# Linear attention and a softplus layer on one core: the sums of keys move from TensorE to VectorE, the last tiles are stored whole, and the order is planned anew

## The chip, the cores and the metric

The kernel runs on one core of a Trainium2 chip. The metric is the time of one execution on the device in microseconds (us). The kernel before took 1017.62 us, the median of 3 runs (1016.76 to 1019.33).

The engines are named as in the profile: PE is TensorE (matrix products), PEld its loading of weights, DVE is VectorE, ACT is ScalarE, POOL is GpSimd, and SP is SyncE, which issues all transfers (DMA) here.

## The reference: what is computed

Eight sequences of 576 tokens, with eight heads of 64 channels, go through an attention with 128 random features, and the result through a layer with a softplus:

```python
def phi(x):
    proj = np.einsum('bhsd,md->bhsm', x, omega)
    sq = np.sum(x * x, axis=-1, keepdims=True) / 2.0
    h = proj - sq
    h = h - np.max(h, axis=-1, keepdims=True)
    return np.exp(h) / np.sqrt(m)
q_p, k_p = (phi(q_s), phi(k_s))
kv = np.einsum('bhsm,bhsd->bhmd', k_p, v)
z = np.sum(k_p, axis=2)
num = np.einsum('bhsm,bhmd->bhsd', q_p, kv)
den = np.einsum('bhsm,bhm->bhs', q_p, z)[..., None] + 1e-06
x = num / den                 # 4608 tokens x 512
h = x @ w_in                  # 512 x 2048
g = np.maximum(h, 0.0) + np.log1p(np.exp(-np.abs(h)))
out = g @ w_out               # 2048 x 512
```

All is float32. `z`, the sum of the key features over the 576 tokens of a sequence, is what the change is about.

## The kernel before

**Tiles.** The work of the attention is cut into 16 quads: a quad is four heads of one sequence (`divmod(n, NQ)` gives the sequence and the half). A quad's 576 tokens are five units, four of 128 tokens and one of 64, and these are worked on as (0, 1), (2, 3) and (4). The first sequence (quads 0 and 1, called early) has its own path, in which `v` carries a column of ones, so that its sums of keys come out of the same products as `kv`. The other 14 quads go as follows.

**Keys.** `plan_unit` loads a unit (L375), projects it (L398) or makes the product from high and low halves (L423), takes the maxima (L448, or L440), and exponentiates on ScalarE (L468, L445). The feature tile `ph` has the tokens on the partitions. In `plan_keys`, `add` (L632, L635, L639) sums the units of a quad element by element into one tile `s` of 128 partitions x 512 columns (four heads x 128 features). What is left is the sum of `s` over its partitions. `burst` makes `kv` in one bank (L562) and, in the other half of that bank, the sums: four products with a broadcast column of ones, `one`, as the stationary side and 128 columns of `s` as the moving side (L663). `scaled` (L583) copies all 512 columns of the bank over `s` on ScalarE, times 1/128; `turn` (L575) transposes the `kv` half of it, and `turned` (L580) copies that to `kvs`. `out_z` (L671) sends the two rows of sums to memory, and `in_z` (L675) reads them back spread to all partitions, as `zb`.

**Queries.** `den` (L784) multiplies the query features with `zb` and sums on VectorE, `invert` (L789) takes the reciprocal, `divide` (L793) scales the features, on GpSimd or VectorE. `flip` (L815) transposes them in 32x32 blocks, into a buffer of the kind `flip`, of which there is one; the result goes out to memory (L822, L826) and back in another arrangement (L838). `num` (L864) makes the products with `kvs`, and the pieces `xh` and `xl` (L878, L884) are the input of the layer, in a ring of two blocks of 512 tokens.

**The layer.** `plan_step` does one of 16 slices of 128 hidden channels for a block of 512 tokens: layer 1 with 12 matmuls (L922 to L924: each float32 product is three matmuls of rounded parts), softplus on ScalarE and VectorE (L928, L931, L934, L937), a split into high and low parts (L941, L945), and layer 2 with 12 matmuls (L951 to L953) into four accumulators. There are nine blocks. At the end of a block, for each of its four tiles of 128 tokens, `left` (L985, VectorE) and `right` (L988, ScalarE) copy half a tile each out of the accumulator, and `store` sends it away. The first eight blocks hold the first 512 tokens of each sequence; a tile there is 128 consecutive rows of the output, in one transfer (L993). The ninth block holds the last 64 tokens of all sequences: a tile is twice 64 rows, of two sequences, and it is stored in two transfers of 64 rows (L996).

**Order.** Nothing is scheduled at run time. Each piece of work is declared by `do` with its engine or engines, an estimated duration, a due time, what it comes after, and which buffers it takes and gives. `in_order` goes through them like a simulation: it takes the engine on which something can start first, and of the works that can start there (nearly) at once, the one that is due first. The result is one order for each engine, which the kernel issues. The due times are offsets to the place of the work in the whole (`FIRST`, `NEXT`, `PACE`, `SPREAD`), all of them numbers in the code. `change` is what the planner adds where TensorE goes from full products to products on half its rows or columns and back, and `GLUE` and `HOLD` let it prefer such works one after the other. In the first 70 us `with_fill` puts matmuls that compute nothing (L1100) into TensorE's gaps. Which semaphore waits a work gets follows from the tiles it reads and writes, not from the planner.

Of the kernel before, what the change touches and what calls it, by code (L numbers as in the profile page):

```python
# [10 lines left out]
F32 = mybir.dt.float32  # L11
# [8 lines left out]
P = 128  # L20
# [166 lines left out]
def favor_softplus_kernel(ctx, tc, q0, k0, qx, kx, tx, vv, om, wi, wo, out):  # L187
# [26 lines left out]
    marks = const.tile([P, 16], F32, name="marks")  # L214
    junk = const.tile([P, 1, M], BF16, name="junk")
# [48 lines left out]
    def plan_weights(nm, fc, due):  # L264
# [36 lines left out]
        def low_part(e):  # L301
# [5 lines left out]
            "SP", 1.46, due + 18.22, load, delay=DL, spare=0 if last else 2,  # L307
# [3 lines left out]
        a = do(("ACT", "DVE"), (aw, dw2), due, low_bits, after=[l], port=True)  # L311
        b = do("ACT", aw, due, rebias, after=[l])
# [33 lines left out]
    def plan_unit(q, kind, us, due, early, other=None):  # L346
# [115 lines left out]
        def exponent(j):  # L462
# [9 lines left out]
            "SP", dma(size), due + 7.17, load, behind=prev.get("load"),  # L472
# [7 lines left out]
        if q.b < SPLIT["t" if tail else kind]:  # L480
            r = do("DVE", dve(w), due - 17.18, norms, after=[s], behind=prev.get("norms"), take=sm)
            prev["norms"] = r
            p = do(
                "PE", 0.02 + 0.224 * nt, due - 86.09, project, after=[ld], mode="r",
# [5 lines left out]
            for j in range(2):  # L490
                e = do(
                    "DVE", dve(n // 2 * M), due - 27.10, lambda j=j: maxima(j), after=[p, e], give=[(b, "x")] if j and not early else [],
                )
            e = do("DVE", dve(n), due - 77.06, less_norms, after=[e], port=True)
            e = do("DVE", dve(n), due - 42.60, bias, after=[e], port=True)
            for j in range(2):
                give = [(b, ("ppb", j))]
                es.append(do(
                    "ACT", n // 2 * 0.25, due + 3.35, lambda j=j: exponent(j), after=[e], behind=es[0] if j else None,
                    give=give + ([(b, "sms")] if j else []),  # L500
                ))
        else:
            hs, ls, l = [], [], None
            for j in range(2):
                h = do(
                    ("ACT", "DVE"), (act(w) + 0.1, dve(w, 2) + 0.115), due - 80.15, lambda e, j=j: high(e, j), after=[ld], behind=hs[-1] if hs else None,
                    take=[] if j else [("sp", b, "sps")], port=True,
                )
                hs.append(h)
                l = do(("DVE", "POOL"), (dve(w) + 0.115, pool(w) + 0.05), due - 101.32, lambda e, j=j: low(e, j), after=[h], behind=l, port=True)  # L510
                ls.append(l)
            r = do("DVE", dve(w), due + 37.54, norms, after=[s] + ls, behind=prev.get("norms"), take=sm, give=[(b, "x")])
            prev["norms"] = r
            e, p = None, prev.get("product")
            for t in range(nt):
                p = do(
                    "PE", 0.236, due - 41.99, lambda t=t: product(t), after=ls, behind=p, take=[(kind_, b, ("ppb", t))],
# [3 lines left out]
                    ("ACT", "DVE"), (act(2 * M, PSUM), dve(2 * M)), due - 52.22, lambda e, t=t: first(e, t), after=[p], behind=e,  # L521
                    take=[] if t else phs,
                )
                e = do("DVE", dve(2 * M), due - 55.00, lambda t=t: second(t), after=[c], give=[(b, ("ppb", t))])
            prev["product"] = p
            e = do("DVE", dve(n * M) + 0.07 * (len(to) - 1), due + 148.43, all_maxima, after=[e, r])
            e = do("DVE", dve(n), due - 58.61, less_norms, after=[e], port=True)
            e = do("DVE", dve(n), due - 61.48, bias, after=[e], port=True)
            es = []
            for t in range(nt):  # L530
                es.append(do(
                    "ACT", 0.587, due - 14.73, lambda t=t: exponents(t), after=[e], behind=es[-1] if es else None,
                    give=[(b, "sms")] if t == nt - 1 else [],
                ))
# [9 lines left out]
        for i in range(len(us)):  # L544
            done.append(plan_queries(q, us[i], due - 31.23 * i, b, es, f"{nm}_{i}", 4 * i))
        plan_flip(q, us, due + 45.54 * (len(us) - 1), b, nm, done)

    def plan_keys(q, us, due, b, es, early):
# [36 lines left out]
        def plan_turn(after, give=[]):  # L585
            old = quads[q.n - 2].nums if q.n >= 2 else []
            t = do("PE", 0.15, due - 20.44, turn, after=[after], take=[(any_, q.slots, "kv")], give=give)
            q.kvl = do(
                ("ACT", "DVE"), (act(2 * M, PSUM), dve(2 * M)), due - 51.46, turned, after=[t] + old,
# [4 lines left out]
        if early:  # L594
# [16 lines left out]
            def first_scaled():  # L611
# [4 lines left out]
                "PE", 0.97 if u < 4 else 0.5, due + 30.74, outer, after=es + [q.kvm], give=[(b, "x")],  # L616
                take=[("acc", q.slots, "kt")] if u == 0 else [],
            )
            if u == 4:
                q.kvl = do(  # L620
                    "ACT", act(4 * D + 4, PSUM), due - 3.61, first_scaled, after=[q.kvm], give=[(q.slots, "kt")],
# [4 lines left out]
        def add(e):  # L626
# [16 lines left out]
            ("POOL", "DVE"), (k * pool(w), k * dve(w)), due - 21.75, add, after=es + [q.sum],  # L643
# [9 lines left out]
        def burst():  # L653
# [5 lines left out]
            z = q.bank[:, 2 * M :].rearrange("p (j m) -> p j m", m=M)  # L659
            for j in range(2):  # L660
                for p in range(2):
                    c = 2 * p + j
                    nc.tensor.matmul(  # L663
                        z[p * D : (p + 1) * D, j], one.broadcast_to([P, D]), q.s[:, c * M : (c + 1) * M],
                        start=False, stop=True, skip_group_check=True,
                    )
# [13 lines left out]
        ldv = do("SP", 1.8, due + 54.76, load_v, take=[("v", q.slots, "v")], delay=DL)  # L680
        q.kvm = do(
            "PE", 0.1 + 0.224 * 12, due - 87.62, burst, after=q.es + [ldv, q.sum], take=[(any_, q.slots, "kt")],
            give=[(x, "phs") for _, x in q.units] + [(q.slots, "v")], mode="c",
        )
        a = do("ACT", act(4 * M, PSUM), due + 14.74, lambda: scaled(4 * M), after=[q.kvm], give=[(q.slots, "kt")])
        t = plan_turn(a)
        r = do("SP", 0.55, due - 15.93, out_z, after=[a], delay=DL)
        q.zc = do(
            "SP", 0.73, due + 95.37, in_z, after=[r, t], take=[("zb", q.slots, "zb")], give=[(q.slots, "s")], delay=DL
        )  # L690

    def plan_first(q, u, due, b, es, nm):
# [51 lines left out]
        def x_low():  # L744
# [3 lines left out]
        t = do("PE", 0.13 * n, due - 136.53, turn, after=es, take=[("any", y, "tp")])  # L748
        h = do(("ACT", "DVE"), (act(n * M, PSUM), dve(n * M)), due - 182.81, turned, after=[t], give=[(y, "tp")])
        a = do(  # L750
            "PE", 0.9, due - 137.59, num, after=[h, q.kvl], take=[("any", y, "nb")], behind=q.nums[-1] if q.nums else None,
            give=[(q.slots, "zb")] if u == NU - 1 else [],
        )
        i = do("DVE", 0.25, due - 82.69, invert, after=[a], take=[("dn", y, "dns")], port=True)
        v = do("DVE", dve(4 * D), due - 90.05, divide, after=[i], give=[(y, "nb"), (y, "dns")])
        k = do("PE", 0.28, due - 68.04, back, after=[v], take=[("any", y, "xb")], give=[(b, "x")])
        q.nums.append(a)
        h = do(
            ("DVE", "ACT"), (dve(2 * w), act(2 * w, PSUM)), due + 32.39, x_high, after=[k], take=[("pt", y, "rs")] if u == 4 else [],
# [5 lines left out]
        l = do("DVE", dve(2 * w), due - 55.33, x_low, after=[h], give=[(y, "xb")])  # L765
# [3 lines left out]
    def plan_queries(q, u, due, bu, es, nm, first):  # L769
# [21 lines left out]
        def divide(e):  # L791
# [4 lines left out]
            "DVE", 1.7 if u < 4 else 1.3, due + 51.88, den, after=es + [q.zc], take=[("dn", b, "dns")],  # L796
            give=[(q.slots, "zb")] if u == NU - 1 else [], port=True,
        )
        d = do("DVE", 0.09, due - 62.30, invert, after=[d])
        return do(("POOL", "DVE"), (1.0 * f, dve(n * M)), due + 165.15, divide, after=[d], give=[(b, "dns")], port=True)  # L800

    def plan_flip(q, us, due, bu, nm, done):
# [25 lines left out]
        def back():  # L828
# [12 lines left out]
            "DVE", dve(n * M), due + 11.73, flip, after=done, give=[(bu, "phs")], take=[("flip", b, "vs")], port=True,  # L841
        )
        o = do("SP", 0.6 * n_out, due + 22.70, away, after=[t], give=[(b, "vs")], delay=DL, take=[("fd" if u < 4 else "ft", b, "ds")])
        h = do(
            "SP", 0.6 * n_in, due + 68.16, back, after=[o], delay=DL, behind=prev.get("turn"),
# [8 lines left out]
    def plan_x(q, due, t0, w, any_, qt):  # L854
# [27 lines left out]
        def x_low(p):  # L882
# [4 lines left out]
            "PE", 0.00342 * w + 0.02, due - 97.01, num, after=qt["works"] + [q.kvl],  # L887
# [4 lines left out]
        for p in range(2):  # L892
            h = do(
                ("DVE", "ACT"), (dve(m) + extra, act(m, PSUM) + extra), due - 41.29, lambda e, p=p: x_high(e, p),
                after=[a] + old_reads(t0, m), behind=h,
            )
            l = do("DVE", dve(m), due - 78.05, lambda p=p: x_low(p), after=[h], give=[(y, ("bank", p))])
# [14 lines left out]
    def plan_step(i, t0, n, fc, due, acc, box):  # L912
# [44 lines left out]
        for ccs in ((0, 1), (2, 3)):  # L957
            a = do(
                "PE", 0.70 if n < TB else 1.36, due, lambda ccs=ccs: layer1(ccs), after=[x for cc, x in need if cc in ccs] + [done_w["i", fc]], behind=a,
# [3 lines left out]
        s = do("ACT", act(n, PSUM), due - 38.85, magnitude, after=[a], take=[("u", b, "us")])  # L963
# [244 lines left out]
```

## Time and profile before

| | |
|---|---|
| median of 3 runs | 1017.62 us |
| the profiled execution | 1017.05 us |
| its span, first to last instruction | 1015.3 us |
| granted TensorE clock, mean | 0.998 |
| PE busy | 998.2 us, 98% |
| DVE busy | 717.6 us, 71% |
| ACT busy | 671.3 us, 66% |
| POOL busy | 180.8 us, 18% |
| transfers | 113.78 MB, mean 112 GB/s |

The profile is of one execution. A row of a group names the line of the kernel, the engine, the operation, what it writes and reads, its shape and how often it comes; then busy time and mean nanoseconds of one, and the idle time of its engine just before it with what ended it. A row of a stage gives its start and end, its length, the busy time of PE, PEld, DVE, ACT and POOL with the number of instructions, the granted clock, the mean busy share of the core's 16 DMA engines, and what they moved in GB/s. A row of a wait names who waited for whom: total, times, longest. A row of one line's or one tile's instructions gives shortest, median and longest duration in ns, and first and last start. Matmuls are pipelined: the duration of one is longer than the time for which it holds the engine.

### The profile page before, as it was taken

How to read it: one execution, taken by the hardware profiler on the slowest of the kernel's cores; microseconds unless marked ns; L12 is line 12 of the kernel's file. 1: busy time of each engine (PE TensorE's matmuls, PEld its weight loads, DVE VectorE, ACT ScalarE, POOL GpSimd, SP SyncE). 2: the span in 40 equal slices, each digit the busy share in tenths (PEclk: the TensorE clock that was granted, in tenths of full speed). 3: DMA queues.
4: the chain of work that ended last, by engine and by line, in shares of the span. 5: the costliest groups of instructions: out<-in, count | busy, mean ns of one | idle time of the engine just before them, and what ended most of it. 6: DMA issues, size and time to landing. Idle time of an engine off the chain costs nothing. (4 is left out here: it accounts for less than half of the span.)

```text
span 1015.3 us, 16615 instructions
## 1 busy us (share of the span) xinstructions
PE 998.2 (98%) x5574; PEld 797.7 (79%) x5574; DVE 717.6 (71%) x1880; ACT 671.3 (66%) x1590; POOL 180.8 (18%) x178
## 2 busy tenths in 40 slices
PE   9999999999999999999999999999999999999997
PEld 8777777777777777778778777878778788888886
DVE  7999888888778877778697878787888333223222
ACT  6999777767676767666676767676766444444442
POOL 2123422221123121212041312311212000000000
PEclk9999999999999999999999999999999999999999
DMA  9667354343433333342534243534231301001001
GB/s 354 233 247 265 101 166 135 130 122 116 127 126 126 93 109 104 121 131 73 151 115 149 76 130 104 160 95 128 82 124 47 96 21 42 1 1 42 1 1 41
DMA packets 64172, 113.78 MB, mean 112 GB/s; under 512 B 18236, under 2 KB 36824, under 8 KB 64088
## 3 DMA queue, kind: packets, MB, share of 16 engines
q1 hardware_dynamic: 64088, 112.73, 34.9%
q8 instruction: 44, 0.72, 0.3%
q14 instruction: 40, 0.33, 0.1%
HBM read 85.68 MB, written 27.03 MB: 111 GB/s over the span
## 5 line engine op out<-in xcount | busy, mean ns | idle before, releaser
L951 PE MATMUL acc<-wo,gh 128*128 128x512 f32 x576 | 230.4, 400 | 1.0 <-ACT o L988 1.0
L922 PE MATMUL h<-xh,wi 128*128 128x512 f32 x576 | 228.8, 397 | 1.8 <-DVE u L937 1.8
L923 PE MATMUL h<-xl,wi 128*128 128x512 f32 x576 | 225.3, 391 | 0.6 <-DVE xl L884 0.3
L952 PE MATMUL acc<-wo,gh 128*128 128x512 f32 x576 | 225.2, 391 | 0.0
L953 PE MATMUL acc<-wo,gl 128*128 128x512 f32 x576 | 224.6, 390 | 0.0
L924 PE MATMUL h<-xh,wi 128*128 128x512 f32 x576 | 224.4, 390 | 0.0
L937 DVE SCALAR_TENSOR_TENSOR u<-h,u 128x512 f32<-128x512 f32 x144 | 98.3, 683 | 134.9 <-ACT u L934 134.2
L928 ACT ACTIVATE u<-h 128x512 f32<-128x512 f32 x144 | 86.3, 600 | 161.3 <-PE h L924 152.1
L951 PEld LDWEIGHTS acc<-wo,gh 128*128 128x128 f32 x576 | 108.1, 188 | 32.8 <-issue 9.7
L922 PEld LDWEIGHTS h<-xh,wi 128*128 128x128 f32 x576 | 108.2, 188 | 29.8 <-issue 4.1
L953 PEld LDWEIGHTS acc<-wo,gl 128*128 128x128 f32 x576 | 108.1, 188 | 23.6 <-DVE gl L945 0.2
L924 PEld LDWEIGHTS h<-xh,wi 128*128 128x128 f32 x576 | 108.2, 188 | 23.2
L923 PEld LDWEIGHTS h<-xl,wi 128*128 128x128 f32 x576 | 108.2, 188 | 21.5 <-DVE xl L884 0.6
L952 PEld LDWEIGHTS acc<-wo,gh 128*128 128x128 f32 x576 | 108.4, 188 | 19.0
L941 ACT CAST gh<-u 128x512 fp32r<-128x512 f32 x123 | 76.1, 620 | 53.6 <-PE acc L952 44.4
L945 POOL TENSOR_TENSOR gl<-u,gh 128x512 fp32r<-128x512 f32 x43 | 57.9, 1347 | 230.0 <-ACT gh L941 145.9
L934 ACT ACTIVATE u<-u 128x512 f32<-128x512 f32 x144 | 91.5, 635 | 3.9
L784 DVE CUSTOM_DVE_ANT_0 junk<-phq,zb 128x128 bf16<-128x128 f32 (+1 forms) x228 | 80.5, 353 | 18.2 <-ACT phq L445 3.0
L931 ACT ACTIVATE u<-u 128x512 f32<-128x512 f32 x144 | 91.6, 636 | 2.6
L945 DVE TENSOR_TENSOR gl<-u,gh 128x512 fp32r<-128x512 f32 x101 | 70.7, 701 | 23.1 <-ACT gh L941 22.2
L468 ACT ACTIVATE phk<-ppk,smk 128x128 f32<-128x128 f32 x230 | 63.5, 382 | 22.4 <-DVE smk L460 22.3
L445 ACT ACTIVATE phq<-phq,smq 128x128 f32<-128x128 f32 x194 | 61.9, 394 | 9.6 <-DVE smq L460 9.6
(129 smaller groups left out, 1325.9 us busy)
## 6 DMA issues: line engine op xcount, KB each, us to landing
xk<-kx SPq DMA_DIRECT2D x28, 512.0 KB, 3.6
xq<-qx SPq DMA_DIRECT2D x28, 512.0 KB, 5.3
fdq<-flq SPq DMA_DIRECT2D x28, 512.0 KB, 2.9
qq<-fdq SPq DMA_DIRECT2D x112, 128.0 KB, 3.1
rawi<-wi SPq DMA_DIRECT2D x16, 512.0 KB, 8.4
rawo<-wo SPq DMA_DIRECT2D x16, 512.0 KB, 7.1
out<-o SPq DMA_DIRECT2D x32, 256.0 KB, 2.2
v<-vv SPq DMA_DIRECT2D x14, 576.0 KB
```

Source lines behind the costliest of these rows:

```text
L784: nc.vector.tensor_tensor_reduce(jk[r, c % jk.shape[1]], ph[r, c], q.zb[r, h], 1.0, 1e-6, ALU.mult, ALU.add, dn[r, 0, c : c + 1])
L922: nc.tensor.matmul(b["h"], wh, xh[:, cc, t], start=cc == 0, stop=False)
L923: nc.tensor.matmul(b["h"], wh, xl[:, cc, t], start=False, stop=False)
L924: nc.tensor.matmul(b["h"], wl, xh[:, cc, t], start=False, stop=cc == NCC - 1)
L928: nc.scalar.activation(b["u"], b["h"], AF.Abs)
L931: nc.scalar.activation(b["u"], b["u"], AF.Exp, scale=-1.0)
L934: nc.scalar.activation(b["u"], b["u"], AF.Ln, bias=1.0)
L937: nc.vector.scalar_tensor_tensor(b["u"], b["h"], 0.0, b["u"], ALU.max, ALU.add)
L945: (nc.vector if e == "DVE" else nc.gpsimd).tensor_tensor(b["gl"], b["u"], b["gh"].bitcast(F32), ALU.subtract)
L951: nc.tensor.matmul(acc[tt], gh, w2[fc][:, 0], start=fc == 0, stop=False)
L952: nc.tensor.matmul(acc[tt], gh, w2[fc][:, 1], start=False, stop=False)
L953: nc.tensor.matmul(acc[tt], gl, w2[fc][:, 0], start=False, stop=fc == NFC - 1)
```

## The change

The four products with ones leave `burst`. In their place `s` is transposed on VectorE in 32x32 blocks into a new tile `st` (in the one `flip` buffer), reduced over 32 columns to 16, and, in a small tile `few` that is cleared once at the start, transposed again and added over the four groups of 32 partitions. `out_z` then sends 16 rows of 32 numbers from `few`. `scaled` copies only the 256 columns of `kv`, and comes after the first transpose, since it writes over columns of `s` that the transpose reads.

The tiles of the last block are stored with one transfer each, whose destination is an access pattern of 2 x 64 x 512. For them the planner takes ScalarE's copy as ready with the accumulator and not after VectorE's copy; the copies themselves are the same.

The planner's durations for some works, its due times and its other settings have new numbers.

```diff
-AHEAD = 264.67
+AHEAD = 312.45
-SLOW = 6.04
+SLOW = 10.94
-PATIENCE = {"PE": 0.00, "DVE": 0.00, "ACT": 0.18, "POOL": 15.27, "SP": 5.65}
-LEAN = {"DVE": 0.27, "POOL": 0.00, "ACT": 0.00}
-SPREAD = ((0, 10.51), (13, 28.11))
+PATIENCE = {"PE": 0.00, "DVE": 0.02, "ACT": 0.17, "POOL": 15.27, "SP": 4.12}
+LEAN = {"DVE": 0.56, "POOL": 0.00, "ACT": 0.00}
+SPREAD = ((0, 10.51), (17, 8.16))
-GLUE = 0.00
-HOLD = 0.00
-START_PACE = 5.87
-EARLY_Q = 0.74
+GLUE = 67.48
+HOLD = 0.09
+START_PACE = 5.26
+EARLY_Q = 7.20
...
+    few = const.tile([P, 2, 32], F32, name="few")
...
+    nc.gpsimd.memset(few, 0.0)
...
             products(*units[-1], q.v[:, 16:])
-            z = q.bank[:, 2 * M :].rearrange("p (j m) -> p j m", m=M)
-            for j in range(2):
-                for p in range(2):
-                    c = 2 * p + j
-                    nc.tensor.matmul(
-                        z[p * D : (p + 1) * D, j], one.broadcast_to([P, D]), q.s[:, c * M : (c + 1) * M],
-                        start=False, stop=True, skip_group_check=True,
-                    )
...
+        def flip_sums():
+            q.st = at.tile([P, 4 * M], F32, name=f"st{q.nm}", tag=q.slots["st"], bufs=1)
+            nc.vector.transpose(q.st, q.s)
+
+        def sums():
+            nc.vector.tensor_reduce(few[:, 0, : 4 * M // 32], q.st.rearrange("p (j t) -> p j t", t=32), AX.X, ALU.add)
+
+        def last_sums():
+            a, b = few[:, 0], few[:, 1]
+            nc.vector.transpose(b, a)
+            nc.vector.tensor_tensor(a[:D], b[:D], b[D:], ALU.add)
+            nc.vector.tensor_tensor(b[:32], a[:32], a[32:D], ALU.add)
+            nc.vector.tensor_scalar(b[:32], b[:32], rm, None, ALU.mult)
+
         def out_z():
-            q.zd = dram.tile([2, 2 * M], F32, name=f"zd{q.nm}", tag="zd", bufs=2)
-            nc.sync.dma_start(q.zd, q.s[0 : 2 * D : D, 2 * M :])
+            q.zd = dram.tile([4 * M // 32, 32], F32, name=f"zd{q.nm}", tag="zd", bufs=2)
+            nc.sync.dma_start(q.zd, few[: 4 * M // 32, 1])
...
-        a = do("ACT", act(4 * M, PSUM), due + 14.74, lambda: scaled(4 * M), after=[q.kvm], give=[(q.slots, "kt")])
-        t = plan_turn(a)
-        r = do("SP", 0.55, due - 15.93, out_z, after=[a], delay=DL)
-        q.zc = do(
-            "SP", 0.73, due + 95.37, in_z, after=[r, t], take=[("zb", q.slots, "zb")], give=[(q.slots, "s")], delay=DL
+        z = do(
+            "DVE", dve(4 * M), due - 33.63, flip_sums, after=[q.sum], take=[("flip", q.slots, "st"), ("few", q.slots, "few")], port=True,
         )
+        a = do("ACT", act(2 * M, PSUM), due - 46.64, lambda: scaled(2 * M), after=[q.kvm, z], give=[(q.slots, "kt")])
+        plan_turn(a, [(q.slots, "s")])
+        z = do("DVE", dve(4 * M), due + 5.39, sums, after=[z], give=[(q.slots, "st")])
+        z = do("DVE", 0.55, due - 98.77, last_sums, after=[z], port=True)
+        r = do("SP", 0.55, due - 30.52, out_z, after=[z], give=[(q.slots, "few")], delay=DL)
+        q.zc = do("SP", 0.73, due + 123.44, in_z, after=[r], take=[("zb", q.slots, "zb")], delay=DL)
...
-                for j in range(2):
-                    nc.sync.dma_start(out[(2 * u + j + 1) * S - D : (2 * u + j + 1) * S, :], o["t"][j * D : (j + 1) * D])
-
-            a = do("DVE", 0.34, due + 0.15, left, after=[ends[tt]], take=[("end" if last else "t2", o, "s")])
-            r = do("ACT", 0.27, due - 75.97, right, after=[a], give=[(box, ("acc", i, tt))])
-            do("SP", 0.75 if t0 < B * MAIN else 1.5, due + 0.04, store, after=[a, r], give=[(o, "s")], delay=2.0)
+                nc.sync.dma_start(out.rearrange("(b s) d -> b s d", s=S)[2 * u : 2 * u + 2, S - D :, :], o["t"])
+
+            a = do("DVE", 0.34, due - 2.24, left, after=[ends[tt]], take=[("end" if last else "t2", o, "s")])
+            r = do("ACT", 0.27, due - 105.06, right, after=[ends[tt]] if last else [a], behind=a if last else None, give=[(box, ("acc", i, tt))])
+            do("SP", 0.75, due - 38.80, store, after=[a, r], give=[(o, "s")], delay=2.0)
...
-    FIRST = 109.77
-    NEXT = 61.17
-    PACE = 1.82
+    FIRST = 102.61
+    NEXT = 89.06
+    PACE = 3.07
```

Some 40 further lines change only a duration or a due time (the planner's duration of a half of layer 1 goes from 1.36 to 1.375 us, of a quarter of layer 2 from 0.684 to 0.692, of the burst from 0.1 + 0.224 x 12 to 0.1 + 0.224 x 10).

More of the change, by code (lines that the diff above doesn't have):

```diff
@@ L306, in plan_weights @@
         l = do(
-            "SP", 1.46, due + 18.22, load, delay=DL, spare=0 if last else 2,
+            "SP", 1.46, due + 31.61, load, delay=DL, spare=0 if last else 2,
             take=[({"i": "qh", "o": "ql"}[nm] if last else "w", box, "raw")],
@@ L310, in plan_weights @@
         aw, dw, dw2, pw = act(DM), dve(DM), dve(DM, 2), pool(DM)
-        a = do(("ACT", "DVE"), (aw, dw2), due, low_bits, after=[l], port=True)
-        b = do("ACT", aw, due, rebias, after=[l])
+        a = do(("ACT", "DVE"), (aw + 0.035, dw2), due, low_bits, after=[l], port=True)
+        b = do("ACT", aw + 0.03, due, rebias, after=[l])
         c = do("DVE", dw, due, joined, after=[a, b], port=True)
@@ L471, in plan_unit @@
         ld = do(
-            "SP", dma(size), due + 7.17, load, behind=prev.get("load"),
+            "SP", dma(size), due + 15.20, load, behind=prev.get("load"),
             take=[("w" if early else "x", b, "x")], delay=DL, spare=2 if early else 0,
@@ L480, in plan_unit @@
         if q.b < SPLIT["t" if tail else kind]:
-            r = do("DVE", dve(w), due - 17.18, norms, after=[s], behind=prev.get("norms"), take=sm)
+            r = do("DVE", dve(w), due + 10.58, norms, after=[s], behind=prev.get("norms"), take=sm)
             prev["norms"] = r
             p = do(
-                "PE", 0.02 + 0.224 * nt, due - 86.09, project, after=[ld], mode="r",
+                "PE", 0.02 + 0.224 * nt, due - 96.65, project, after=[ld], mode="r",
                 behind=prev.get("project"),
@@ L491, in plan_unit @@
                 e = do(
-                    "DVE", dve(n // 2 * M), due - 27.10, lambda j=j: maxima(j), after=[p, e], give=[(b, "x")] if j and not early else [],
+                    "DVE", dve(n // 2 * M), due - 36.44, lambda j=j: maxima(j), after=[p, e], give=[(b, "x")] if j and not early else [],
                 )
-            e = do("DVE", dve(n), due - 77.06, less_norms, after=[e], port=True)
-            e = do("DVE", dve(n), due - 42.60, bias, after=[e], port=True)
+            e = do("DVE", dve(n), due - 37.34, less_norms, after=[e], port=True)
+            e = do("DVE", dve(n), due - 45.13, bias, after=[e], port=True)
             for j in range(2):
@@ L498, in plan_unit @@
                 es.append(do(
-                    "ACT", n // 2 * 0.25, due + 3.35, lambda j=j: exponent(j), after=[e], behind=es[0] if j else None,
+                    "ACT", n // 2 * 0.25, due - 0.03, lambda j=j: exponent(j), after=[e], behind=es[0] if j else None,
                     give=give + ([(b, "sms")] if j else []),
@@ L505, in plan_unit @@
                 h = do(
-                    ("ACT", "DVE"), (act(w) + 0.1, dve(w, 2) + 0.115), due - 80.15, lambda e, j=j: high(e, j), after=[ld], behind=hs[-1] if hs else None,
+                    ("ACT", "DVE"), (act(w) + 0.1, dve(w, 2) + 0.115), due - 4.01, lambda e, j=j: high(e, j), after=[ld], behind=hs[-1] if hs else None,
                     take=[] if j else [("sp", b, "sps")], port=True,
@@ L509, in plan_unit @@
                 hs.append(h)
-                l = do(("DVE", "POOL"), (dve(w) + 0.115, pool(w) + 0.05), due - 101.32, lambda e, j=j: low(e, j), after=[h], behind=l, port=True)
+                l = do(("DVE", "POOL"), (dve(w) + 0.115, pool(w) + 0.2), due - 76.28, lambda e, j=j: low(e, j), after=[h], behind=l, port=True)
                 ls.append(l)
-            r = do("DVE", dve(w), due + 37.54, norms, after=[s] + ls, behind=prev.get("norms"), take=sm, give=[(b, "x")])
+            r = do("DVE", dve(w), due + 30.96, norms, after=[s] + ls, behind=prev.get("norms"), take=sm, give=[(b, "x")])
             prev["norms"] = r
@@ L516, in plan_unit @@
                 p = do(
-                    "PE", 0.236, due - 41.99, lambda t=t: product(t), after=ls, behind=p, take=[(kind_, b, ("ppb", t))],
+                    "PE", 0.236, due - 9.84, lambda t=t: product(t), after=ls, behind=p, take=[(kind_, b, ("ppb", t))],
                     give=[(b, "sps")] if t == nt - 1 else [],
@@ L531, in plan_unit @@
                 es.append(do(
-                    "ACT", 0.587, due - 14.73, lambda t=t: exponents(t), after=[e], behind=es[-1] if es else None,
+                    "ACT", 0.587, due - 50.02, lambda t=t: exponents(t), after=[e], behind=es[-1] if es else None,
                     give=[(b, "sms")] if t == nt - 1 else [],
@@ L586, in plan_turn @@
             old = quads[q.n - 2].nums if q.n >= 2 else []
-            t = do("PE", 0.15, due - 20.44, turn, after=[after], take=[(any_, q.slots, "kv")], give=give)
+            t = do("PE", 0.15, due - 81.14, turn, after=[after], take=[(any_, q.slots, "kv")], give=give)
             q.kvl = do(
-                ("ACT", "DVE"), (act(2 * M, PSUM), dve(2 * M)), due - 51.46, turned, after=[t] + old,
+                ("ACT", "DVE"), (act(2 * M, PSUM), dve(2 * M)), due + 3.70, turned, after=[t] + old,
                 give=[(q.slots, "kv")],
@@ L615, in plan_keys @@
             q.kvm = do(
-                "PE", 0.97 if u < 4 else 0.5, due + 30.74, outer, after=es + [q.kvm], give=[(b, "x")],
+                "PE", 0.97 if u < 4 else 0.5, due + 9.14, outer, after=es + [q.kvm], give=[(b, "x")],
                 take=[("acc", q.slots, "kt")] if u == 0 else [],
@@ L620, in plan_keys @@
                 q.kvl = do(
-                    "ACT", act(4 * D + 4, PSUM), due - 3.61, first_scaled, after=[q.kvm], give=[(q.slots, "kt")],
+                    "ACT", act(4 * D + 4, PSUM), due - 59.41, first_scaled, after=[q.kvm], give=[(q.slots, "kt")],
                     take=[("zb", q.slots, "zb")],
@@ L642, in plan_keys @@
         q.sum = do(
-            ("POOL", "DVE"), (k * pool(w), k * dve(w)), due - 21.75, add, after=es + [q.sum],
+            ("POOL", "DVE"), (k * pool(w), k * dve(w) + 0.2), due - 71.26, add, after=es + [q.sum],
             take=[("s", q.slots, "s")] if u == 0 else [], port=True,
@@ L764, in plan_first @@
             return
-        l = do("DVE", dve(2 * w), due - 55.33, x_low, after=[h], give=[(y, "xb")])
+        l = do("DVE", dve(2 * w), due + 7.12, x_low, after=[h], give=[(y, "xb")])
         for p in range(2):
@@ L840, in plan_flip @@
         t = do(
-            "DVE", dve(n * M), due + 11.73, flip, after=done, give=[(bu, "phs")], take=[("flip", b, "vs")], port=True,
+            "DVE", dve(n * M), due + 20.79, flip, after=done, give=[(bu, "phs")], take=[("flip", b, "vs")], port=True,
         )
-        o = do("SP", 0.6 * n_out, due + 22.70, away, after=[t], give=[(b, "vs")], delay=DL, take=[("fd" if u < 4 else "ft", b, "ds")])
+        o = do("SP", 0.6 * n_out, due + 53.49, away, after=[t], give=[(b, "vs")], delay=DL, take=[("fd" if u < 4 else "ft", b, "ds")])
         h = do(
-            "SP", 0.6 * n_in, due + 68.16, back, after=[o], delay=DL, behind=prev.get("turn"),
+            "SP", 0.6 * n_in, due + 4.59, back, after=[o], delay=DL, behind=prev.get("turn"),
             take=[] if qt["works"] else [("q", qt, "tag")], give=[(b, "ds")],
@@ L958, in plan_step @@
             a = do(
-                "PE", 0.70 if n < TB else 1.36, due, lambda ccs=ccs: layer1(ccs), after=[x for cc, x in need if cc in ccs] + [done_w["i", fc]], behind=a,
+                "PE", 0.73 if n < TB else 1.375, due, lambda ccs=ccs: layer1(ccs), after=[x for cc, x in need if cc in ccs] + [done_w["i", fc]], behind=a,
                 take=[] if ccs[0] else [("h", b, "hs")],
```

68 lines of the change are left out of this document (34 added, 34 removed).

## The prediction

> **What bounds the kernel now.** I read the head of the page first, then busy time by stage, then what TensorE (PE) waited for.
>
> ```profile
> span 1015.3 us, 16615 instructions
> PE 998.2 (98%) x5574; PEld 797.7 (79%) x5574; DVE 717.6 (71%) x1880; ACT 671.3 (66%) x1590; POOL 180.8 (18%) x178
> ```
>
> ```profile
> 70.00:90.00 20.00, 20.00 (x126) 15.90 (x125) 19.48 (x52) 19.78 (x46) 6.46 (x6) 1.00 0.86 317
> ...
> 200.00:300.00 100.00, 99.86 (x577) 78.88 (x576) 81.73 (x227) 67.38 (x172) 21.30 (x21) 1.00 0.39 117
> ...
> 950.00:1000.00 50.00, 50.00 (x222) 41.42 (x221) 12.51 (x19) 23.29 (x38) 0.00 (x0) 1.00 0.00 1
> 1000.00:1016.00 16.00, 8.83 (x39) 6.96 (x38) 3.72 (x7) 2.74 (x6) 0.00 (x0) 0.87 0.30 66
> ```
>
> ```profile
> PE ppq L423 <- DVE xl L884: 2.0, 2, 1.2
> PE h L922 <- DVE u L937: 1.8, 3, 0.9
> PE fill L1100 <- ACT xq L705: 1.1, 1, 1.1
> ```
>
> In the stages the columns after the length are busy PE, PE weight load, DVE, ACT and POOL, then clock, DMA share and GB/s. From about 70 us to its last matmul PE has no room: 99.86 of 100 us in the middle, 50 of 50 at the end. VectorE (DVE) is behind it, at 82% in the middle, with 97% only in the lead (19.48 of 20). PE's longest single wait is 1.2 us. So in the body time is set by how much PE has to do, and then a tail follows in which PE does nothing: it works 8.83 of the last 16 us. That tail in order of time, and in slices of half a microsecond:
>
> ```profile
> 1007.68 5.00 SPq L996 DMA_DIRECT2D out<-o  x8
> ...
> 1008.44 0.39 PE L953 MATMUL acc<-wo,gl 128*128 128x512 f32 x1
> 1008.70 0.37 ACT L988 COPY o<-acc 128x256 f32<-128x256 f32 x1 [0.31 <-DVE o L985]
> 1008.87 0.42 DVE L985 COPY o<-acc 128x256 f32<-128x256 f32 x1 [0.25 <-PE acc L953]
> 1009.33 0.37 ACT L988 COPY o<-acc 128x256 f32<-128x256 f32 x1 [0.25 <-DVE o L985]
> ```
>
> ```profile
> 1008.50:1009.00 0.50, 0.33 (x2) 0.00 (x0) 0.25 (x2) 0.30 (x1) 0.00 (x0) 1.00 0.27 66
> ...
> 1010.00:1010.50 0.50, 0.00 (x0) 0.00 (x0) 0.00 (x0) 0.00 (x0) 0.00 (x0) 1.00 0.94 209
> ...
> 1013.50:1014.00 0.50, 0.00 (x0) 0.00 (x0) 0.00 (x0) 0.00 (x0) 0.00 (x0) 0.50 0.86 184
> 1014.00:1014.50 0.50, 0.00 (x0) 0.00 (x0) 0.00 (x0) 0.00 (x0) 0.00 (x0) 0.50 0.02 4
> ```
>
> PE ends at 1008.44 + 0.39 = 1008.83; the span ends 6.5 us later. The last copy is over at 1009.70, and what is left is DMA alone: four tiles of 256 KB in eight halves (1.05 MB) move from about 1008.87 (a share of 0.27 in that half microsecond is 0.13 us at full) to 1014.0, with the engines some nine tenths busy; then 1.3 us to the end.
>
> **Sums of keys leave TensorE.** For each of 14 quads the four products with `one` go, which the trace shows as eight matmuls.
>
> ```profile
> L663 PE MATMUL kt<-s,marks x112: 272/273/273, 69.3 to 756.7; 128*64 128x128 f32 x112
> L583 ACT ACTIVATE s<-kt x14: 581/597/599, 70.7 to 757.6; 128x512 f32<-128x512 f32 x14
> ```
>
> ```profile
> 756.55 0.44 PE kt L663 x8
> ```
>
> The 273 ns are with the pipeline's depth; what eight of them hold up is the 0.44 us of the chain of waits. PE is full at the places from 69 to 757 us, so 14 x 0.44 = **6.2 us** come off the path. The products left in the burst are the same on both sides of the gap, so no further change of array shape goes or comes. ScalarE's `scaled` copies 256 columns instead of 512: 597 ns against 0.37 us for a copy of 128x256 in the tail, 14 x 0.22 = 3.1 us, beside PE's work: nothing on the path.
>
> **What VectorE gets.** Per quad a transpose of 128x512, a reduction of 128x512 to 16, and four small operations.
>
> ```profile
> L815 DVE STREAM_TRANSPOSE flq<-phq 128x1024 f32<-128x1024 f32 x28 | 34.7, 1240 | 0.5
> L388 DVE TENSOR_REDUCE smk<-xk 128x8 f32<-128x512 f32 x28 | 19.0, 678 | 1.7 <-POOL xk L383 1.0 <-ACT xk L381 0.7
> L815 DVE STREAM_TRANSPOSE flq<-phk 128x256 f32<-128x256 f32 x13 | 5.8, 443 | 5.9 <-DMA fdq<-flq 5.8
> L460 DVE SCALAR_TENSOR_TENSOR smk<-smk 128x8 f32<-128x8 f32 x28 | 4.4, 158 | 0.5
> ```
>
> Transpose: a third of the way from 443 to 1240, 0.71. Reduction 0.68. Small ones 4 x 0.16 = 0.64. Together 2.0 us, times 14 = 28 us, between 70 and 760 us: 4 us in each 100, so DVE goes from 82 to 86 of 100. It lies beside PE's work as long as 14 us of each 100 are free; the cover is gone in the lead, where one or two quads (2 to 4 us) meet a DVE that is 97% busy. The new wait is there too: `scaled` overwrites the part of `s` that the transpose reads, so ScalarE waits for DVE, and behind it in ScalarE's queue stand the softplus steps of layer 1 (L928, L931, L934) on which PE's layer 2 waits. The transpose takes the one `flip` buffer, where the flips already wait 5.8 us in all for a DMA to land.
>
> The sums leave for memory behind DVE's work and no longer behind the burst and `scaled`; SP's later loads stand behind that issue, and PE's waits above name no DMA, so I count nothing. The clearing of `few` falls on POOL at the start, which is 18% busy: nothing. That the plan takes the last ScalarE copies as free of DVE's costs and gains nothing, as the two copies themselves are not edited (in the tail each waits for the other, 0.25 us).
>
> **The new order.** Its due times can't be read as time. In the lead, gaps of PE are filled with matmuls that compute nothing, and these count as busy:
>
> ```profile
> L1100 PE MATMUL fill<-ident 128*128 128x128 f32 x56 | 8.5, 290 | 1.1 <-ACT xq L705 1.1
> ```
>
> Bounds: PE stands still 1008.83 - 998.2 = 10.6 us before its last matmul and is filled for 8.5, so no order gains more than 19.1; if each of the 14 quads got one wait as long as PE's longest now, it would lose 14 x 1.2 = 16.8. I take **0**, in the middle of small waits on both sides, and 8 us either way for most of it.
>
> **The last tiles stored whole.** Eight halves, each a run of 64 rows, become four stores of 128 rows. The source has 128 partitions; the destination is now `[2, 64, 512]`, with the 2 outermost, since the two runs of 64 rows lie in different sequences. What the outermost count does must be read from the transfers there are.
>
> ```profile
> DMA packets 64172, 113.78 MB, mean 112 GB/s; under 512 B 18236, under 2 KB 36824, under 8 KB 64088
> ```
>
> ```profile
> xk<-kx SPq DMA_DIRECT2D x28, 512.0 KB, 3.6
> ...
> fdq<-flq SPq DMA_DIRECT2D x28, 64.0 KB, 2.3
> ...
> rest<-r SPq DMA_DIRECT2D x16, 64.0 KB, 2.8
> ...
> zd<-s SPq DMA_DIRECT2D x14, 2.0 KB
> ...
> omf<-om SPq DMA_DIRECT2D x1, 64.0 KB
> ```
>
> The 22 rows of which these are the first and the last count 448 transfers. Packets under 512 B: the two groups with rows of 256 B have (28 + 16) x 256 = 11264 of 18236, which leaves 6972. Sixteen to each transfer (one closing packet for each of 16 engines, as I read it) would be 7168; 196 are missing, 14 x 14. That is the 14 transfers `zd<-s`, whose source is two partitions: two engines each instead of sixteen. It is the only transfer with an outermost count under 16, and the nearest row to a store with a 2 outermost. So I take two engines for the new stores, 64 rows of 2 KB on each.
>
> The Trainium skill, "DMA: Bandwidth & Descriptors", section "Why a DMA increments its semaphore by 16 and not by 1", says that a transfer runs on the largest number of engines up to 16 that divides the slowest dimension of both sides; by it the new store gets two. The same page's list of choices (the row on two transfers to disjoint partition halves) advises one transfer of 128 partitions instead of two halves; by that alone the sum would be the 1008.4 below. `zd<-s` agrees with the first; no run here yet shows a 2 outermost with many rows under it.
>
> The price, from whole tiles in the middle of the run and from the tail now:
>
> ```profile
> 930.50:931.00 0.50, 0.50 (x4) 0.42 (x3) 0.50 (x1) 0.00 (x0) 0.00 (x0) 1.00 1.02 385
> ```
>
> 385 GB/s at a share of 1.02 is 23.6 GB/s for one engine, so 64 rows (131,072 bytes) take 5.55 us. In the tail now, 209 GB/s at 0.94 is 13.9 GB/s, or 9.4 us; there sixteen engines read 64 partitions at once, which two don't, so I take 5.55. All four stores come ready within 2 us, on the same two engines: 4 x 5.55 = 22.2 us from 0.04 after PE's end, then 1.3: a tail of 23.5 instead of 6.5, **+17.0 us**.
>
> **Sum.** The profiled execution took 1017.05 (its span and 1.75 around it), 0.57 under the median of the runs shown. 1017.05 - 6.2 + 0 + 17.0 = 1027.9; I say **1028**.
>
> **The rivals.** *Sixteen engines after all* (spread by the number of rows, which `zd<-s`, with two rows, doesn't exclude): then the last store is issued at 0.89 after PE's end, begins 1.2 later (1007.68 to 1008.87), takes 0.7 (256 KB at the 385 GB/s above) and 1.3 follow, a tail of 4.1. 1017.05 - 6.2 - 2.4 = 1008.4, faster. It decides from four engines up: the sum stands even with before when the tail is 6.5 + 6.2 = 12.7, which leaves 11.4 us for data, and k engines need 44.4 / k. *Two engines at the tail's rate*: 4 x 9.4 = 37.7, tail 39.0, 1043; against it, the 64 partitions shared by sixteen engines. *The new wait*: ScalarE held by a late transpose in every quad, PE without layer 2 work, 16.8 more on top of two engines: 1045; for it, DVE at 97% in the lead and a single flip buffer; against it, PE's waits on DVE of 1.8 and 2.0 in all with DVE at 82%. That the sums don't leave PE, I see no way for.
>
> **Chances.** Two engines 0.70, as all 448 transfers agree with it and one shows it; sixteen 0.17; two engines at the slow rate 0.06; the new wait 0.07. The likeliest one's own range is 1020 to 1036 (8 us of order either way). The range of 1007 to 1036 takes in the sixteen engines too, and leaves out the two slow rivals. A measurement here tells about 0.3%, 3 us, from no change: 1014.6 to 1020.7. Sixteen engines give nearly all of faster, 0.16; their slow end and the fast end of the likeliest give 0.06 within; the rest, 0.78, is slower.
>
> **What will show it.** PE's group L663 gone and PE's last matmul near 1002.6 (the first step); DVE some 28 us up with PE's waits on DVE and ACT small (the second and the order); four stores issued within 2 us of PE's end, and behind them some 22 us in which the DMA share is about 2/16 at 47 GB/s. If that stretch shows a share of 0.9 and ends within 3 us of the last issue, my tail is wrong, and the time is near 1008; if PE ends after 1012, the order or the new wait is.

## The result, and the profile after

The changed kernel took 1033.24 us, the median of 4 runs (1030.81 to 1033.53), against 1018.48 us (4 runs, 1016.76 to 1019.36): a ratio of 1.0142, 95% interval 1.012 to 1.0164. It is slower by some 14.5 us; the forecast was 1028, and the median lies 5.2 us over it. Its profiled execution took 1030.81, with a span of 1029.0; it is the fastest of the four. All ratios below are to the kernel before, run beside on the same chip (its medians there are 1018.05 to 1018.18); the brackets are 95% intervals. A ratio is not exactly the quotient of the two medians.

The head of its page, and its stages (columns as before: busy PE, PEld, DVE, ACT, POOL, then clock, DMA share, GB/s):

```profile
span 1029.0 us, 16459 instructions
PE 990.7 (96%) x5436; PEld 791.2 (77%) x5436; DVE 713.0 (69%) x1860; ACT 684.5 (67%) x1638; POOL 240.3 (23%) x235
```

```profile
150.00:200.00 50.00, 44.09 (x243) 33.24 (x242) 42.51 (x109) 35.65 (x92) 14.36 (x15) 0.93 0.50 150
200.00:300.00 100.00, 100.00 (x562) 78.78 (x561) 76.94 (x209) 70.90 (x178) 32.80 (x31) 1.00 0.36 109
...
950.00:1000.00 50.00, 50.00 (x222) 41.41 (x221) 12.46 (x18) 22.83 (x37) 0.00 (x0) 1.00 0.00 1
1000.00:1030.00 30.00, 5.17 (x23) 3.94 (x21) 2.39 (x5) 1.66 (x5) 0.00 (x0) 0.66 0.10 35
```

PE is full in the middle and at the end, as before, and then works 5.17 of the last 30 us. The end in order of time, and in stretches:

```profile
1004.03 10.23 SPq L1006 DMA_DIRECT2D out<-o  x4
...
1004.79 0.39 PE L964 MATMUL acc<-wo,gl 128*128 128x512 f32 x1
1005.05 0.37 ACT L999 COPY o<-acc 128x256 f32<-128x256 f32 x1 [0.36 <-DVE o L996]
1005.21 0.42 DVE L996 COPY o<-acc 128x256 f32<-128x256 f32 x1 [0.26 <-PE acc L964]
1005.67 0.37 ACT L999 COPY o<-acc 128x256 f32<-128x256 f32 x1 [0.25 <-DVE o L996]
```

```profile
1006.00:1008.00 2.00, 0.00 (x0) 0.00 (x0) 0.00 (x0) 0.04 (x1) 0.00 (x0) 1.00 0.13 31
1008.00:1012.00 4.00, 0.00 (x0) 0.00 (x0) 0.00 (x0) 0.00 (x0) 0.00 (x0) 0.71 0.13 50
...
1020.00:1024.00 4.00, 0.00 (x0) 0.00 (x0) 0.00 (x0) 0.00 (x0) 0.00 (x0) 0.50 0.13 51
1024.00:1028.00 4.00, 0.00 (x0) 0.00 (x0) 0.00 (x0) 0.00 (x0) 0.00 (x0) 0.50 0.10 39
```

PE ends at 1004.79 + 0.39 = 1005.18, 3.7 us earlier than before; the tail is 23.8 us instead of 6.5. For 20 us the sixteen DMA engines are busy for 0.13 of their time, which is two of sixteen, at 51 GB/s.

What VectorE got, and what TensorE waited for:

```profile
L665 DVE STREAM_TRANSPOSE st<-s 128x512 f32<-128x512 f32 x14 | 9.8, 702 | 2.1 <-DMA fdq<-flq 2.1
...
L668 DVE TENSOR_REDUCE few<-st 128x16 f32<-128x512 f32 x14 | 9.6, 684 | 0.2
...
L672 DVE STREAM_TRANSPOSE few<-few 128x32 f32<-128x32 f32 x14 | 2.9, 209 | 0.4
...
L673 DVE TENSOR_TENSOR few<-few 64x32 f32<-64x32 f32 x14 | 2.6, 188 | 0.5
...
L674 DVE TENSOR_TENSOR few<-few 32x32 f32<-32x32 f32 x14 | 2.5, 180 | 0.5
L675 DVE TENSOR_SCALAR few<-few 32x32 f32<-32x32 f32 x14 | 2.4, 170 | 0.5
```

```profile
L585 ACT ACTIVATE s<-kt 128x256 f32<-128x256 f32 x14 | 5.4, 383 | 8.7 <-PE kt L564 7.5 <-DVE st L665 1.2
```

```profile
PE acc L962 <- ACT gh L952: 4.4, 1, 4.4
PE kt L564 <- DVE xl L895: 2.4, 1, 2.4
PE ppq L425 <- DVE phq L438: 1.2, 3, 0.6
```

The new work is 29.8 us of VectorE, yet its total didn't rise (717.6 before, 713.0 now): the new order gives more to GpSimd, 240.3 us instead of 180.8. ScalarE's copy of `kv` (L585) waited 1.2 us in all for the transpose. Two single waits of TensorE, of 2.4 us near 107 us and 4.4 us near 160 us, are new.

The packets answer the count that the prediction made:

```profile
DMA packets 64445, 113.78 MB, mean 111 GB/s; under 512 B 18536, under 2 KB 37096, under 8 KB 64360
```

There are 444 transfers now, four stores for eight. `zd` has 16 rows and so 14 x 16 packets of 128 B. With 11264 packets of 256 B, sixteen closing packets for each of 440 transfers and two for each of the four stores, the sum is 11264 + 224 + 7040 + 8 = 18536, the page's number exactly.

### The profile page after: what moved, and what is told of

Same layout as the page of the kernel before. It is cut to its first block, busy times and chain, and to the rows that moved or that the text cites. A ratio compares the mean times of both kernels' runs of the same rounds, so it can differ in the third digit from the quotient of the medians.

```text
span 1029.0 us, 16459 instructions
## 1 busy us (share of the span) xinstructions
PE 990.7 (96%) x5436; PEld 791.2 (77%) x5436; DVE 713.0 (69%) x1860; ACT 684.5 (67%) x1638; POOL 240.3 (23%) x235
## 2 busy tenths in 40 slices
DMA packets 64445, 113.78 MB, mean 111 GB/s; under 512 B 18536, under 2 KB 37096, under 8 KB 64360
## 4 chain that ended last, share of the span: by engine, by line
PE 76%; DVE 10%; ACT 5%; DMA 4%; issue 2%; POOL 0%; SPq 0%; DVEq 0%; ACTq 0%
PE acc L962 11%; PE h L933 11%; PE h L934 11%; PE h L935 11%; PE acc L963 11%; PE acc L964 11%; PE kt L564 3%; PE ppk L400 3%; PE xp L875 2%; PE ppq L425 2%; DVE junk L795 2%; DMA xq<-q 1%; DMA xq<-qx 1%; DVE flq L826 1%; DVE u L948 1%
## 5 line engine op out<-in xcount | busy, mean ns | idle before, releaser
L956 POOL TENSOR_TENSOR gl<-u,gh 128x512 fp32r<-128x512 f32 x51 | 66.4, 1302 | 231.6 <-ACT gh L952 185.6
L956 DVE TENSOR_TENSOR gl<-u,gh 128x512 fp32r<-128x512 f32 x93 | 66.6, 716 | 25.6 <-ACT gh L952 24.0
L804 POOL TENSOR_TENSOR phq<-phq,dnq 128x512 f32<-128x512 f32 (+1 forms) x57 | 64.0, 1136 | 54.7 <-DVE dnq L800 35.3
```

What stands on the lines that cost most here:

```text
L956: (nc.vector if e == "DVE" else nc.gpsimd).tensor_tensor(b["gl"], b["u"], b["gh"].bitcast(F32), ALU.subtract)
```

## Experiments: the store of the last tiles

**Halves again, in the changed kernel.** The two lines of before come back in `store`:

```diff
-                nc.sync.dma_start(out.rearrange("(b s) d -> b s d", s=S)[2 * u : 2 * u + 2, S - D :, :], o["t"])
+                for j in range(2):
+                    nc.sync.dma_start(out[(2 * u + j + 1) * S - D : (2 * u + j + 1) * S, :], o["t"][j * D : (j + 1) * D])
```

> The changed kernel, with the last four tiles stored as before, in eight halves of 64 rows. If the store with 2 outermost carries the loss, the tail after the last matmul goes from 23.8 us back to 6.5 us, and the time from 1033.2 to about 1016 (its profiled execution from 1030.8 to 1013.5), near the kernel before or under it. If the loss lies in the order or in VectorE's new work, the time stays above 1028.

Measured: 1015.79 us (10 runs), ratio 0.9982 (0.9968 to 0.9996), with a tail of 6.5 us. The rest of the change, by itself, is faster by 1.8 us by the ratio (0.4 to 3.3 by its interval). The store costs 17.4 us by the medians (1033.24 - 1015.79) and 16.3 by the ratios (1.0142 - 0.9982).

**That store alone, in the kernel before.** The same edit the other way round, with the old order and the sums on TensorE.

> The kernel before, with nothing but the store of the last tiles changed to one transfer of 2 x 64 x 512 each. If that store alone costs what the tail showed, the time is 1018 + 17.3 = 1035, with a DMA share of 0.125 for about 21 us after the last matmul. If the long tail needs the new order or the new sums, the time stays at 1018.

Measured: 1033.65 us (4 runs), ratio 1.0158 (1.0142 to 1.0173), which is 16.1 us, with a tail of 23.4 us. Of its stretches after the last matmul:

```profile
1012.00:1016.00 4.00, 0.00 (x0) 0.00 (x0) 0.00 (x0) 0.00 (x0) 0.00 (x0) 0.50 0.13 51
...
1024.00:1028.00 4.00, 0.00 (x0) 0.00 (x0) 0.00 (x0) 0.00 (x0) 0.00 (x0) 0.50 0.13 51
```

Undoing it in one kernel and doing it in the other agree within 2 us: the store is the loss, and it needs nothing else of the change.

**Is it the outermost count?** One transfer of 128 rows and a destination in two levels came together with the 2. In the next kernels the tokens of the last block stand in another order inside a tile, which `plan_rest` arranges when it reads them back, so that the same 128 rows of 2 KB go out with another outermost count:

```diff
-                nc.sync.dma_start(out.rearrange("(b s) d -> b s d", s=S)[2 * u : 2 * u + 2, S - D :, :], o["t"])
+                nc.sync.dma_start(out.rearrange("(b s) d -> s b d", s=S)[S - D :, 2 * u : 2 * u + 2, :], o["t"])
...
+    def in_tiles(x):
+        return x.rearrange("c (u j r) -> c u r j", u=4, j=2)
+
+    def to_tiles(x):
+        return x.rearrange("c (u r j) -> c u r j", u=4, j=2)
...
-                    (nc.scalar.copy if e == "ACT" else nc.vector.tensor_copy)(xh[x], b["t"][:, p])
+                    (nc.scalar.copy if e == "ACT" else nc.vector.tensor_copy)(to_tiles(xh[x]), in_tiles(b["t"][:, p]))
...
-                    nc.vector.tensor_tensor(xl[x], b["t"][:, p], xh[x].bitcast(F32), ALU.subtract)
+                    nc.vector.tensor_tensor(to_tiles(xl[x]), in_tiles(b["t"][:, p]), to_tiles(xh[x].bitcast(F32)), ALU.subtract)
```

> The changed kernel, with the tokens of the last block in another order inside a tile (row r of the two sequences side by side), so that the same tile of 128 rows goes out in one transfer whose destination is 64 x 2 x 512: 64 outermost instead of 2, the same bytes and the same rows of 2 KB. If the outermost count sets how many engines work, all sixteen do: a tail of about 4.1 us, a time of 1033.2 - 19.7 = 1013.5, the DMA share at 0.9. If a destination in two levels as such, or one transfer of 128 rows, is what makes it slow, it stays at 1033.

> The kernel before with the same store of 64 x 2 x 512, and the sums still on TensorE and the old order. If sixteen engines move whole tiles, the tail goes from 6.5 to about 4.1 us and the time from 1018 to 1015.6. If whole tiles gain nothing over halves, 1018.

Measured: in the changed kernel 1014.44 us (6 runs), ratio 0.9964 (0.9949 to 0.998), with a tail of 4.8 us; in the kernel before 1016.65 (10 runs), ratio 0.9982 (0.997 to 0.9995), with a tail of 4.5 us. The end of the first of them:

```profile
1008.00:1009.00 1.00, 0.00 (x0) 0.00 (x0) 0.42 (x1) 0.59 (x2) 0.00 (x0) 1.00 0.92 340
1009.00:1010.00 1.00, 0.00 (x0) 0.00 (x0) 0.00 (x0) 0.00 (x0) 0.00 (x0) 1.00 1.03 383
1010.00:1011.00 1.00, 0.00 (x0) 0.00 (x0) 0.00 (x0) 0.00 (x0) 0.00 (x0) 1.00 0.87 326
```

The destination still has two levels and the transfer still has 128 rows; with 64 outermost it runs on all engines at 383 GB/s. So neither of those made it slow. Two counts between, with tiles of four and of eight sequences (`[4 * g : 4 * g + 4, s0 : s0 + 32, :]` with `s0 = S - D + 32 * h`, and `[:, s0 : s0 + 16, :]` with `s0 = S - D + 16 * u`):

> The changed kernel with tiles of the last block made of 16 rows from each of eight sequences, stored in one transfer of 8 x 16 x 512: 8 outermost. Two engines moved 51 GB/s together, so 25.5 each; eight move 204 GB/s, and four tiles (1.05 MB) take 5.1 us with a DMA share of 0.5. With the 3.2 us that lay around the data in the tail of 2 outermost, a tail of 8.3 us, against 23.8 with 2 and 4.8 with 64 outermost. If anything but the outermost count decides, the tail is 4.8 or 23.8.

> The changed kernel with tiles of the last block made of 32 rows from each of four sequences, stored in one transfer of 4 x 32 x 512: 4 outermost. Four engines at 25.5 GB/s move 102 GB/s: 10.3 us for the four tiles at a DMA share of 0.25, and a tail of about 13.5 us, between 23.8 (2 outermost) and 9.0 (8 outermost). If the engines don't follow the outermost count, it stands near one of these two.

Measured, in a single execution each: 1019.29 us with a tail of 9.0 us (eight) and 1025.74 us with a tail of 14.3 us (four), each tail some 0.7 us over what was expected. Four, then eight:

```profile
1014.00:1016.00 2.00, 0.00 (x0) 0.00 (x0) 0.00 (x0) 0.00 (x0) 0.00 (x0) 0.50 0.26 102
```

```profile
1011.00:1012.00 1.00, 0.00 (x0) 0.00 (x0) 0.00 (x0) 0.00 (x0) 0.00 (x0) 1.00 0.51 180
```

| outermost | DMA share | GB/s | tail, us |
|---|---|---|---|
| 2 | 0.13 | 51 | 23.8 |
| 4 | 0.26 | 102 | 14.3 |
| 8 | 0.51 | 180 | 9.0 |
| 64 | 1.03 | 383 | 4.8 |

The shares are 2, 4, 8 and 16 sixteenths to within 0.03. The packets say the same without any time: those under 512 B are 18536, 18544, 18560 and 18592 in the four kernels. Without the closing packets of the four last stores the count above gives 18528, so the four stores close with 8, 16, 32 and 64 packets: 2, 4, 8 and 16 engines each. The number of engines follows the outermost count of the destination.

## Experiments: the sums of keys and the order

All four are made from the changed kernel with the store of 64 outermost, in the same planned order, so that one thing at a time differs. That reference was run in the section above (0.9964), and once more beside the kernel without VectorE's new work:

> The changed kernel with the store of 64 x 2 x 512 once more, as the reference for the next run on the same chip: 1014.4, ratio 0.9964 to the kernel before.

Measured: 1013.25 us (11 runs), ratio 0.9956 (0.9942 to 0.997). Together the reference is 0.9956 to 0.9964.

**The products in addition.** The eight removed lines with `one` are back in `burst`; nothing reads their results.

```diff
+            z = q.bank[:, 2 * M :].rearrange("p (j m) -> p j m", m=M)
+            for j in range(2):
+                for p in range(2):
+                    c = 2 * p + j
+                    nc.tensor.matmul(
+                        z[p * D : (p + 1) * D, j], one.broadcast_to([P, D]), q.s[:, c * M : (c + 1) * M],
+                        start=False, stop=True, skip_group_check=True,
+                    )
```

> The changed kernel with the store of 64 x 2 x 512 and the four products with ones done in every burst as well, in the same order of work; their results are not read. If TensorE's own time sets the body, they cost 14 x 0.44 = 6.2 us: 1020.6. If the products had lain in time that PE had to wait anyway, nothing: 1014.4.

Measured: 1019.32 us (12 runs, 1016.61 to 1023.12), ratio 1.0009 (0.9996 to 1.0022), 0.0045 to 0.0053 over the reference, which is 4.6 to 5.4 us. By the intervals that is known to some 2 us either way. So they did lie on the path; the 6.2 lies a little higher, but not beyond the intervals.

**VectorE's work left out**, first without and then with the transpose of 128x512:

```diff
-    nc.gpsimd.memset(few, 0.0)
+    nc.gpsimd.memset(few, 1.0)
...
         def flip_sums():
-            q.st = at.tile([P, 4 * M], F32, name=f"st{q.nm}", tag=q.slots["st"], bufs=1)
-            nc.vector.transpose(q.st, q.s)
+            pass
...
         def sums():
-            nc.vector.tensor_reduce(few[:, 0, : 4 * M // 32], q.st.rearrange("p (j t) -> p j t", t=32), AX.X, ALU.add)
+            pass
...
         def last_sums():
-            a, b = few[:, 0], few[:, 1]
-            nc.vector.transpose(b, a)
-            nc.vector.tensor_tensor(a[:D], b[:D], b[D:], ALU.add)
-            nc.vector.tensor_tensor(b[:32], a[:32], a[32:D], ALU.add)
-            nc.vector.tensor_scalar(b[:32], b[:32], rm, None, ALU.mult)
+            pass
```

> The changed kernel with the store of 64 x 2 x 512, in the same order, with the reduction and the four small operations left out, so that the sums of keys are ones and the denominators are wrong; the first transpose stays, and so does what waits for it. VectorE has 14 x 1.4 = 20 us less. If its new work lies beside PE's, the time stays within 1.5 us of 1014.4; if it holds PE up, 4 us or more come back: 1010 or less.

> The same, in the same order, with all of VectorE's new work left out, the transpose of 128x512 too, so that the sums of keys are ones and the denominators are wrong, and ScalarE's copy of kv no longer waits for VectorE. Leaving out the reduction and the four small operations gave 1011.9 against 1014.4 on another chip, 2.5 us for 20 us of VectorE. If that is VectorE's load, the whole of it (2.1 us a quad, 30 us) gives about 3.7: 1010.7. If it is ScalarE's wait for the transpose that costs, another 4 or more come: 1007. If the 2.5 us were the spread of the runs, it stays at 1014.4, within 1 us of the reference.

Measured: 1011.85 us (6 runs), ratio 0.9943 (0.993 to 0.9956) without the five later operations, and 1012.38 (7 runs), ratio 0.9952 (0.9934 to 0.9971), without any of it. The first fell between the two expectations. The second shows no more: 0.9 us by the medians, 0.4 us by the ratios, against a reference on the same chip, inside both intervals. So VectorE's 30 us lie beside PE's work, and neither they nor ScalarE's wait for the transpose cost anything that these runs can tell from nothing, which is about 2 us.

The traces of both also tell where the two new waits of TensorE come from. They are there, as long as ever, when all of VectorE's new work is left out:

```profile
PE acc L957 <- ACT gh L947: 4.4, 1, 4.4
PE kt L564 <- DVE xl L890: 2.4, 1, 2.4
```

So they belong to the new order (which the planner made with this work in it), and not to the time that the work takes.

**The gap near 160 us.**

```diff
-        for w in with_fill(*in_order(works, room, AHEAD, MARGIN), room["any"], 70, fill):
+        for w in with_fill(*in_order(works, room, AHEAD, MARGIN), room["any"], 200, fill):
```

> The changed kernel with the store of 64 x 2 x 512 (median 1014.4, ratio to before 0.9964), and the matmuls that compute nothing put into planned gaps up to 200 us of the plan instead of 70. In the order PE stands for 4.4 us near 160 us, and the granted clock is 0.5 for 6.8 us after it. If the gap is one that the plan itself leaves, and the clock falls because PE stands, the clock stays at 1.0 after it, and 6.8 x 0.5 = 3.4 us come back: near 1011. If the clock falls for another reason, or the gap is no planned one, the time stays at 1014.4.

The gap in the changed kernel, and the same place with the filling:

```profile
160.00:165.00 5.00, 0.89 (x16) 0.70 (x14) 4.84 (x14) 2.30 (x7) 2.13 (x3) 0.81 0.63 210
165.00:170.00 5.00, 4.67 (x20) 3.11 (x22) 4.79 (x14) 3.59 (x12) 0.00 (x0) 0.50 0.02 4
```

```profile
164.06 3.62 PE L1116 MATMUL fill<-ident 128*128 128x128 f32 x30
167.84 0.50 PE L962 MATMUL acc<-wo,gh 128*128 128x512 f32 x1 [0.17 <-ACT gh L952]
```

```profile
160.00:165.00 5.00, 5.00 (x38) 4.10 (x37) 4.95 (x10) 3.87 (x9) 2.60 (x3) 1.00 0.46 172
165.00:170.00 5.00, 4.34 (x30) 3.45 (x29) 4.90 (x14) 1.42 (x5) 0.61 (x1) 1.00 0.44 137
```

Measured: 1012.91 us (5 runs), ratio 0.995 (0.9938 to 0.9961). The gap was the plan's own (the filling found it), and with PE at work in it the clock stays at 1.00. Of the time, 0.6 to 1.4 us by the ratios come back, known to some 2 us; the expected 3.4 lies at the edge of that or beyond. Whether the clock cost less than thought or PE then waits elsewhere stays open. It is the fastest complete version here, 5 us under the kernel before; its lead over the reference is not beyond the intervals.

## Why the prediction was right, and where it was off

- **The store, right, and its mechanism.** +17.0 was forecast; the tail grew by 23.8 - 6.5 = 17.3. The choice of two engines rested on one kind of transfer, `zd<-s`, with two rows; the table above bears it out with 2, 4, 8 and 64. The price was a little off: an engine alone moves 51 / 2 = 25.5 GB/s, not 23.6, and the data (1.05 MB at 51 GB/s) took 20.6 us, not 22.2; beside the data the tail has 3.2 us, where 1.3 were forecast. The two errors, of 1.6 and 1.9 us, cancel; that the sum came within 0.3 us is luck, the number of engines is not. The rival of two engines at the tail's rate, 13.9 GB/s each, falls by the same 25.5. The rule of the Trainium skill ("DMA: Bandwidth & Descriptors", section "Why a DMA increments its semaphore by 16 and not by 1") holds in all four; all four counts are powers of two, so no run here tests the part of it on divisors. The advice of the Trainium skill on that page for one transfer of 128 partitions holds here only where the outermost count lets it: 383 GB/s with 64, 51 with 2, against 209 for the halves in the tail before.
- **Sixteen engines, fallen.** Its number of 1008.4 would have been too low in any case: with 64 outermost the tail is 4.8, near the forecast 4.1, and yet the kernel takes 1013 to 1014.
- **The sums off PE, right.** 6.2 was forecast, 4.6 to 5.4 measured, to some 2 us. That the size was a little high is likely and not shown.
- **VectorE at nothing, right.** The six operations take 0.702 + 0.684 + 0.209 + 0.188 + 0.180 + 0.170 = 2.13 us a quad, 2.0 forecast, and cost nothing that the runs can tell. That VectorE would be 28 us busier was wrong: the new plan gives GpSimd 59.5 us more, and VectorE is busy for 77 of 100 us in the middle, where 86 were forecast. So the cover was wider than the one that the forecast argued with. The rival of the new wait falls: in all 14 quads ScalarE waited 1.2 us for the transpose, once.
- **The order at 0, off by about +3.** With the halves the rest of the change gains 1.8 us, where the sums alone gain some 5. The difference of 3 us is worked out, not isolated, and each of its two parts is known to 1.5 or 2 us. The two waits of 4.4 and 2.4 us, which stay without VectorE's new work, are where the trace shows PE standing; the 0 in the middle was a guess, and its 8 us either way held it. In sum the profiled execution was forecast at 1027.9 and took 1030.8: 0.3 from the tail, 2.6 from PE's end (1005.2 for 1002.6). The median lies another 2.4 us higher.

## What to carry to other kernels

Look at the outermost count of a transfer, on the side of the destination too, and not at its size or its partitions alone: fewer and larger transfers lost 16 to 17 us here because of a 2 in front, and the same bytes with 64 in front gained 1.4 to 1.8 over the halves. Order the data so that the large count is outermost; here it took two rearranged reads. Where PE is full, taking products off it did pay, some 5 us, and the engine with time to spare did their work at no cost that showed; but the whole of the sums and the new order gained only 1.8.

## What the runs showed beside this

The granted clock falls for a shorter stand of PE than I had thought of. After the 4.4 us wait it was at half for about 6.9 us (0.81 and 0.50 in the two stretches above: 1.9 + 5.0). The 2.4 us wait near 107 us lowered the clock too in eight of the ten profiles of the changed order, and not in the other two, with the same wait and the same order up to there. The changed kernel, then the one with 64 outermost:

```profile
105.00:110.00 5.00, 2.65 (x15) 1.68 (x13) 4.89 (x13) 2.86 (x7) 4.52 (x6) 1.00 0.01 2
110.00:115.00 5.00, 5.00 (x62) 4.09 (x62) 4.43 (x17) 4.97 (x11) 1.03 (x2) 1.00 0.29 89
```

```profile
105.00:110.00 5.00, 2.74 (x13) 1.61 (x9) 4.90 (x13) 2.84 (x7) 4.52 (x5) 1.00 0.00 2
110.00:115.00 5.00, 4.90 (x44) 4.21 (x45) 4.59 (x18) 3.82 (x8) 1.19 (x2) 0.66 0.00 0
```

In the second the clock is at half for 0.34 / 0.5 x 5 = 3.4 us. The two profiled executions without the drop, that of the changed kernel and that without VectorE's new work, are the fastest of their runs (1030.81 where the others took 1032.96 to 1033.53, and 1009.32 of 1009.32 to 1014.65). That may be part of why runs of the changed order differ by some us among themselves; no run isolates it. The Trainium skill ("TensorE: Matmul & The Clock Gate", section "Why this matters for your kernels") advises to leave no gap of PE over some 3 us; the 4.4 us agrees, and 2.4 us were enough here in eight of ten profiles.
